# Window attention and gated feed-forward on one core: weight loads ahead of casts, value tiles held back, half turns one to a slot, query copies on ScalarE

## The chip, the core and the metric

The kernel runs on one core of a Trainium2 chip. The metric is the device time of one execution in microseconds. Executions of one kernel agreed within about 1% here (263.0 to 265.9 us for most runs of the kernel before), so differences are read from rounds in which both kernels ran on the same chip. Medians are over all runs of a round; where a slow one is among them, this is said. The changed kernel was timed in one round only, so an experiment is set against it across rounds; the kernel before had medians of 264.65, 264.78, 264.01 and 264.18 us in the four rounds, so less than about 1 us between rounds decides nothing.

## The reference

Four batches of eight heads, 768 positions, 64 columns a head. Each position attends to the first 4 positions and to the last 128. A feed-forward part follows, with a relu gate.

```python
scores = scale * np.matmul(q, k.transpose(0, 1, 3, 2))
keep = is_sink | in_window                  # 4 sinks, window of 128
a = softmax(np.where(keep, scores, -1e9))   # written out in the original
attn = np.matmul(a, v)                      # (4, 8, 768, 64)
x = attn.transpose(0, 2, 1, 3).reshape(3072, 512)
out = (np.maximum(x @ w_gate, 0) * (x @ w_val)) @ w_out    # d_ff = 1536
```

## The kernel before

The feed-forward part of a batch is 24 *slots*: two halves of the positions (g = 0, 1) by twelve column blocks of 128 (m). A slot is one `chunk`: four matmuls for the gate, four for the value, a relu on ScalarE and a product on VectorE (`hT`). Attention work of the same or the next batch is put behind the chunks by a plan: `S` is one group of scores with its exp and mask, `V` the sums, the division and the value product of one pair of heads, `T` the turn of keys and queries to head-dimension-major form, `H` the turn of the second half of batch 0's positions. "V01" is pair 0, part 1 (the second half); the chunks of g = 1 need all four V of part 1.

```python
def chunk(b, g, m):
    gp, vp = G[gvn[0] % 3], G[(gvn[0] + 1) % 3]         # three banks in turn
    ...  # 4 matmuls with wg into gp
    nc.scalar.activation(gs[:], gp[:, 0:CUT], Act.Relu, bias=0.0, scale=1.0)
    ...  # 4 matmuls with wv into vp
    nc.vector.tensor_tensor(h[:, m, c], gs[:], vp[:, 0:CUT], op=Alu.mult)

def V(u, part):
    x = V1(u, part)     # sums with ones
    V3(*x[:3])          # values: vn, tile by tile
    V4(*V2(*x))         # division and product on VectorE, into xT
```

The weights are cast while they are loaded, and GpSimd asks for them; it also casts the value tiles (`vf` to `vn`) and the halves of keys and queries, all in one order. SyncE asks for the float32 tiles. (To *ask* for a load is to issue its DMA.) In the profile's lines `qT` and `kE` are the turned queries and keys, `ee` the exps, `xT` the attention output, `hT` the product of a chunk, `wg` and `wv` the gate and value weights, `g` and `pp` banks of PSUM. L282 are the scores, L298 the sums and the value products, L340 and L345 the gate and value matmuls of a chunk, L131 the casts of value tiles.

```python
cast_v(0, 1)
cast_v(0, 2)
...
cast_half(3, (nc.gpsimd.tensor_copy, nc.scalar.copy))
Sg(U[2], 0)
load_w(0, 2)                    # gate and value weights of blocks 0 and 1
...
load_w(2, 4)
load_half(6)
load_half(7)
for j in (3, 4, 5, 6):          # the value tiles of part 1
    load_v(0, j, 16 if j == 3 else 0)
...
prep[1] += [("half", 6), ("half", 7), ("v", 0, 3), ("v", 0, 4), ("w", 6, 8), ("v", 0, 5), ("v", 0, 6),
            ("w", 8, 10), ("w", 10, 12)]
```

The softmax here doesn't subtract the row's maximum and nothing guards it: scores larger than these inputs give would overflow.

Of the kernel before, what the change touches and what calls it, by code (L numbers as in the profile page):

```python
# [19 lines left out]
def kernel(  # L20
# [12 lines left out]
    nc = tc.nc  # L33
# [19 lines left out]
    vf = const.tile([128, 7, H, 64], F32, name="vf")  # L53
# [66 lines left out]
    def load_v(b, j, r0=0, r1=128):  # L120
        r1 = min(r1, S - VROW[j])

        parts = [(0, 4, 0), (4, 16, VROW[j] + 4), (16, 128, VROW[j] + 16)] if j in (1, 3, 5) else [(0, 128, VROW[j])]
        for a0, a1, s0 in parts:
            a1 = min(a1, r1)
            if r0 <= a0 < a1:
                nc.sync.dma_start(out=vf[a0:a1, j, :, :], in_=v[b, :, s0:s0 + a1 - a0, :].rearrange("h s d -> s h d"))  # L127

    def cast_v(b, j, rows=128, copy=nc.gpsimd.tensor_copy):
        flat = lambda ap: ap.rearrange("p h d -> p (h d)")  # L130
        copy(flat(vn[b % 2][0:rows, j, :, :]), flat(vf[0:rows, j, :, :]))  # L131
# [27 lines left out]
        copy(e[:, 124:892].rearrange("d (i c) -> d i c", c=256)[:, :, 0:4],  # L159
             e[:, 0:4].unsqueeze(1).to_broadcast([128, 3, 4]))  # L160

    def load_w(m0, m1):
        for w, dst in ((moe_w_gate, wg), (moe_w_val, wv)):
            nc.gpsimd.dma_start(out=dst[:, :, m0 * 128:m1 * 128],
                                in_=w.rearrange("(ko ki) n -> ki ko n", ki=128)[:, :, m0 * 128:m1 * 128])

# [64 lines left out]
    def T(u):  # L231
        t = u.i % NT
        tk, tq = two()
        for x, ps in ((kn[u.i % 2], tk), (qn[u.i % 2], tq)):
            for n in range(NR):
                for h in range(2):
                    r = slice(64 * h, 64 * h + 64)
                    nc.tensor.transpose(ps.bitcast(BF16)[r, 64 * n:64 * n + 64], x[r, 64 * n:64 * n + 64], ident[r, r])
        vk, vq = (ps.bitcast(BF16)[:, 0:S].rearrange("d (n p) -> d p n", p=PR) for ps in (tk, tq))
        e = kE[t]  # L240
        to = lambda ap: ap.rearrange("d (p n) -> d p n", n=NR)
        nc.scalar.copy(to(e[:, 0:120]), vk[:, 0:10])
        for i in range(2):
            nc.scalar.copy(to(e[:, 128 + 256 * i:380 + 256 * i]), vk[:, 10 + 21 * i:31 + 21 * i])
        nc.scalar.copy(to(e[:, 640:784]), vk[:, 52:64])
        nc.vector.tensor_copy(to(qT[t][:]), vq)  # L246
        sinks(u, nc.scalar.copy)

    def T_half(c):
# [117 lines left out]
    with tc.manual_schedule():  # L367
        nc.vector.memset(idle[:], 0.0)
        spin(7)
        load_half(0, (nc.sync, nc.scalar))  # L370
        load_half(1, (nc.sync, nc.scalar))
        load_v(0, 0)
        load_v(0, 3, 0, 16)
        load_half(2)
        load_v(0, 1)
        load_v(0, 2)
        for c in range(3, 6):
            load_half(c)
        setup()
        setup2(1)  # L380
        cast_half(0)
        T_half(0)
        spin(2, 1)
        Sg(U[0], 0)
        Sg(U[0], 3)
        cast_half(1)
        T_half(1)
        cast_v(0, 0)
        cast_v(0, 3, 16, nc.vector.tensor_copy)
        x = V1(U[0], 0)  # L390
        v0 = V2(*x)
        Sg(U[1], 0)
        cast_half(2)
        cast_v(0, 1)
        cast_v(0, 2)
        Sg(U[1], 3)
        T_half(2)
        x = V1(U[1], 0)
        v1 = V2(*x)
        V3(*v0[:3])  # L400
        V4(*v0)
        V3(*v1[:3])
        V4(*v1)
        cast_half(3, (nc.gpsimd.tensor_copy, nc.scalar.copy))
        Sg(U[2], 0)
        load_w(0, 2)
        Sg(U[2], 3)
        T_half(3)
        cast_half(4)
        V(U[2], 0)  # L410
        Sg(U[3], 0)
        cast_half(5)
        Sg(U[3], 3)
        load_w(2, 4)
        load_half(6)
        load_half(7)
        for j in (3, 4, 5, 6):
            load_v(0, j, 16 if j == 3 else 0)
        V(U[3], 0)
        T_half(4)  # L420
        setup2(2)
        load_w(4, 6)
        spin(6, 2)
        head[0] = False


        slots = []
        for b in range(B):
            slots += [(b, g, m) for g in range(2) for m in range(FM)]
        plan = [[] for _ in slots]  # L430
        at = {}

        def put(s, y, n):
            st = (y[0], n * NP + int(y[1]), int(y[2]) if len(y) > 2 else 0)
            at[st] = s
            plan[s].append(st)

        for s, w in {0: "S04 S02 H1", 1: "S14 S12", 2: "H2", 3: "S24 S22 H3", 4: "S34 S32", 5: "V01", 6: "V11",
                     7: "V21", 8: "V31"}.items():
            for y in w.split():  # L440
                put(s, y, 0)
        for s, w in {12: "T0", 13: "T1", 14: "S00 S01", 15: "S10 S11", 16: "T2", 17: "S20 S21", 18: "V00",
                     19: "V10 T3", 20: "V20", 21: "S30 S31", 22: "V30 S02"}.items():
            for y in w.split():
                put(s, y, 1)
        for b in range(2, B + 1):
            if b < B:
                w = ("Vp01 Sp12 Vp11 Sp22 Vp21 Sp32 Vp31 Sn00 Sn01 Sn10 "
                     "Vn00 Sn11 Sn20 Vn10 Sn21 Sn30 Vn20 Sn31 Vn30 Sn02")
            else:  # L450
                w = "Vp01 Sp12 Vp11 Sp22 Vp21 Sp32 Vp31"
            for x, y in enumerate(w.split()):
                put(24 * (b - 1) + x // 2 * 2, y[0] + y[2:], b - (y[1] == "p"))
        prep = [[] for _ in slots]
        prep[1] += [("half", 6), ("half", 7), ("v", 0, 3), ("v", 0, 4), ("w", 6, 8), ("v", 0, 5), ("v", 0, 6),
                    ("w", 8, 10), ("w", 10, 12)]
        prep[9] += [("load", 4), ("load", 5), ("load", 6), ("lv", 1)]
        prep[10] += [("kq", 4), ("load", 7), ("kq", 5)]
        prep[13] += [("kq", 6)]
        prep[15] += [("v", 1, j) for j in range(7)]  # L460
        prep[16] += [("kq", 7), ("td", 8), ("wo",)]
        for i in range(ND, len(U)):
            t = at["S", i - NP, 2] + 1
            if i > ND:
                prep[t - 6].append(("td", i))
            prep[t].append(("turn", i))
            prep[at["S", i, 0] - 1].append(("sinks", i))
            assert t < at["S", i, 0] - 2
        for b in range(2, B):
            s0 = at["V", b * NP, 0]  # L470
            prep[s0 - 7].append(("lv", b))
            for j in range(7):
                prep[s0 - 3 + j // 2 if j < 6 else s0].append(("v", b, j))

        f2 = deque()
        for s, (b, g, m) in enumerate(slots):
            for x in prep[s]:
                if x[0] == "kq":
                    cast_kq(U[x[1]])
                elif x[0] == "load":  # L480
                    gate(U[x[1]])
                    load_kq(U[x[1]])
                elif x[0] == "half":
                    cast_half(x[1])
                elif x[0] == "w":
                    load_w(*x[1:])
                elif x[0] == "wo":
                    for c in range(3):
                        load_wo(c)
                elif x[0] == "td":  # L490
                    to_dram(U[x[1]])
                elif x[0] == "turn":
                    turn(U[x[1]])
                elif x[0] == "sinks":
                    sinks(U[x[1]], nc.gpsimd.tensor_copy)
                elif x[0] == "lv":
                    for j in range(7):
                        load_v(x[1], j)
                else:
                    cast_v(*x[1:])  # L500
            chunk(b, g, m)
            for what, i, x in plan[s]:
                if what == "T":
                    T(U[i])
                elif what == "H":
                    T_half(NP + i)
                elif what == "S":
                    Sg(U[i], x)
                else:
                    V(U[i], x)  # L510
            for _ in range(3):
                if f2:
                    f2.popleft()()
            if s == 23:
                f2 += [lambda t=t, mm=mm: ffn2(0, t, mm) for t in range(6) for mm in range(FM)]
            if b > 0 and m == FM - 1:
                f2 += [lambda b=b, t=t, mm=mm: ffn2(b, t, mm) for t in range(3 * g, 3 * g + 3) for mm in range(FM)]
        tail[0] = 1
        while f2:
            f2.popleft()()  # L520
# [35 lines left out]
```

## Time and profile before

| | before |
|---|---|
| median of the first 3 runs | 264.69 us (263.51 to 265.35) |
| profiled span | 261.9 us |
| TensorE busy | 247.7 us (95%) |
| granted TensorE clock | 0.997 |
| first V of part 1 (slot 5) starts | 33.99 us |
| first turn of batch 1 (slot 12) starts | 47.55 us |

In this page each row has one digit for a fortieth of the span (6.5 us): the busy share of TensorE in tenths, and below it the clock that the throttle granted, in tenths of full speed.

```profile
PE   7877899998899999999999999999999999999994
...
PEclk9999999999999999999999999999999999999998
```

Apart from the end, all waits lie in the first 16 slices (the last is at 102.95 us). The first V of part 1, and the casts of the last two value tiles that it uses, timeline of TensorE and of GpSimd:

```profile
33.99 0.54 PE L298 MATMUL pp<-ee,ones 128*64 128x115 bf16 x10
34.38 0.52 PE L298 MATMUL pp<-ee,vn 128*64 128x115 bf16 x10
...
30.34 1.75 POOL L131 CAST vn<-vf 128x512 bf16<-128x512 f32 x2 [1.72 <-DMA vf<-in_v_dram]
```

The casts are done by 32.1, 2 us before V01 starts, and V01 waits for nothing.

### The profile page before, as it was taken

The page shows a single profiled execution, that of the slowest core. Times are in us where ns is not written, and L with a number is a line of the kernel's source. Part 1 is how long each engine was busy: PE and PEld are TensorE (multiplying, and loading weights), DVE is VectorE, ACT ScalarE, POOL GpSimd, SP SyncE. Part 2 cuts the span into 40 slices and gives each one's busy share as a digit, 9 for nine tenths or more (in the row PEclk, how much of TensorE's full clock was granted, in tenths as well). Part 3 has the DMA queues.
Part 4 walks back from the last instruction along what each step waited for, and adds up shares of the span by engine and source line. Part 5 has one row for each costly group of instructions (what it writes and reads, how often), then busy time and mean ns, then how long its engine had stood idle before and what let it go on. Part 6 is the DMA issues. An engine that isn't in the chain of part 4 may idle for free.

```text
span 261.9 us, 5490 instructions
## 1 busy us (share of the span) xinstructions
PE 247.7 (95%) x2143; PEld 140.5 (54%) x2143; DVE 151.2 (58%) x316; ACT 116.5 (44%) x224; POOL 73.0 (28%) x100
## 2 busy tenths in 40 slices
PE   7877899998899999999999999999999999999994
PEld 2454565655555555555555555555555655555441
DVE  7675888487987665657357567667265742323000
ACT  3765742594543454454333464463344233332211
POOL 6791631759960003894000033000000000000000
PEclk9999999999999999999999999999999999999998
DMA  7999997995999969499712393310110011101232
GB/s 192 275 248 191 149 131 194 309 238 56 158 170 155 115 133 203 98 163 145 117 52 62 69 219 85 109 43 0 40 43 7 36 40 40 41 4 40 80 123 80
DMA packets 81266, 30.45 MB, mean 116 GB/s; under 512 B 65368, under 2 KB 77144, under 8 KB 81240
## 3 DMA queue, kind: packets, MB, share of 16 engines
q1 hardware_dynamic: 47944, 21.83, 34.3%
q0 software_dynamic: 32752, 7.87, 34.1%
q8 instruction: 17, 0.28, 0.5%
q10 hardware_dynamic: 544, 0.39, 0.5%
q14 instruction: 9, 0.07, 0.1%
HBM read 28.48 MB, written 9.44 MB: 145 GB/s over the span
## 4 chain that ended last, share of the span: by engine, by line
PE 74%; DMA 8%; DVE 7%; ACT 3%; issue 3%; SPq 2%; POOL 1%; DVEq 0%; ACTq 0%
PE g L360 20%; PE g L340 19%; PE g L345 19%; PE pp L298 7%; DMA vf<-in_v_dram 5%; PE pp L360 4%; PE pp L282 4%; DMA wv<-in_moe_w_val_dram 3%; ACT ee L286 3%; SPq L127 2%; DVE hT L347 2%; DVE t L313 1%; DVE R L315 1%; DVE ee L289 1%; DVE qT L246 1%
## 5 line engine op out<-in xcount | busy, mean ns | idle before, releaser
L347 DVE TENSOR_TENSOR hT<-gs,g 128x384 bf16<-128x384 f32 x96 | 52.8, 550 | 65.5 <-PE g L345 64.7
L340 PE MATMUL g<-xT,wg 128*128 128x384 bf16 x384 | 78.4, 326 | 0.7 <-DVE hT L347 0.5
L345 PE MATMUL g<-xT,wv 128*128 128x384 bf16 x384 | 78.1, 326 | 0.7 <-DMA wv<-in_moe_w_val_dram 0.7
L343 ACT ACTIVATE gs<-g 128x384 f32<-128x384 f32 x96 | 47.4, 494 | 69.1 <-PE g L340 67.2
L360 PE MATMUL g<-wo,hT 128*128 128x512 bf16 x240 | 64.1, 380 | 0.0
L286 ACT ACTIVATE ee<-pp 128x998 bf16<-128x998 f32 (+4 forms) x52 | 45.3, 902 | 34.9 <-PE pp L282 34.8
L340 PEld LDWEIGHTS <-wg 128*128 128x128 bf16 x384 | 36.0, 98 | 32.5 <-issue 2.1
L345 PEld LDWEIGHTS <-wv 128*128 128x128 bf16 x384 | 37.5, 98 | 26.0 <-DMA wv<-in_moe_w_val_dram 1.1
L360 PEld LDWEIGHTS <-hT 128*128 128x128 bf16 x288 | 26.2, 98 | 26.2 <-issue 2.1
L289 DVE TENSOR_TENSOR ee<-ee,msk 128x838 bf16<-128x838 bf16 (+4 forms) x48 | 30.0, 633 | 10.7 <-ACT ee L286 10.6
L131 POOL CAST vn<-vf 128x512 bf16<-128x512 f32 x28 | 18.1, 654 | 39.7 <-DMA vf<-in_v_dram 37.3
L148 POOL DMA_DIRECT2D qd<-in_q_dram x8 | 25.1, 4452 | 0.0
L148 POOL DMA_DIRECT2D kd<-in_k_dram x8 | 22.7, 3910 | 0.3 <-issue 0.3
L282 PE MATMUL pp<-qT,kE 64*128 64x255 bf16 (+6 forms) x240 | 17.2, 246 | 3.7 <-DVE qT L267 1.7
L364 ACT COPY ot<-g 128x512 f32<-128x512 f32 x20 | 11.7, 586 | 18.2 <-PE g L360 17.4
L315 DVE STREAM_TRANSPOSE R<-r 128x384 f32<-128x384 f32 x32 | 18.5, 578 | 1.1
L313 DVE STREAM_TRANSPOSE t<-pp 128x384 f32<-128x384 f32 x28 | 16.2, 580 | 4.1 <-PE pp L298 3.5
L298 PEld LDWEIGHTS <-ones 128*64 128x64 bf16 x288 | 12.6, 109 | 10.4 <-issue 9.8
L323 DVE TENSOR_TENSOR xT<-pp,R 128x384 bf16<-128x384 f32 x28 | 15.6, 557 | 1.0
L282 PEld LDWEIGHTS <-kE 64*128 64x128 bf16 x240 | 8.8, 94 | 11.8 <-issue 8.4
L298 PE MATMUL pp<-ee,ones 128*64 128x115 bf16 (+8 forms) x256 | 14.4, 237 | 0.2
L298 PE MATMUL pp<-ee,vn 128*64 128x115 bf16 (+8 forms) x256 | 13.9, 233 | 0.5 <-POOL vn L131 0.5
(74 smaller groups left out, 129.3 us busy)
## 6 DMA issues: line engine op xcount, KB each, us to landing
out_dram<-ot SPq DMA_DIRECT2D x24, 256.0 KB
vf<-in_v_dram SPq DMA_DIRECT2D x12, 256.0 KB
vf<-in_v_dram SPq DMA_DIRECT2D x12, 224.0 KB
kf<-in_k_dram SPq DMA_DIRECT2D x8, 192.0 KB
wg<-in_moe_w_gate_dram POOLq DMA_DIRECT2D x6, 256.0 KB, 7.2
wv<-in_moe_w_val_dram POOLq DMA_DIRECT2D x6, 256.0 KB, 8.1
kf<-in_k_dram SPq DMA_DIRECT2D x4, 384.0 KB
qf<-in_q_dram SPq DMA_DIRECT2D x4, 384.0 KB
```

Of the source, the lines that this page charges most:

```text
L148: nc.gpsimd.dma_start(out=dst[u.i - ND].rearrange("s (h d) -> s h d", h=2), in_=x[u.b, 2 * u.p:2 * u.p + 2].rearrange("h s d -> s h d"))
L282: nc.tensor.matmul(out=ps[:, h, c0:c1], lhsT=kE[t][64 * h:64 * h + 64, x0:x0 + 128], rhs=qT[t][64 * h:64 * h + 64, q0:q0 + c1 - c0], start ...
L286: nc.scalar.activation(x, ps[:, :, b0:n], Act.Exp, bias=0.0, scale=scale)
L289: nc.vector.tensor_tensor(x, x, msk[:, g, m0:m0 + c1 - c0].unsqueeze(1).to_broadcast([128, 2, c1 - c0]), op=Alu.mult)
L298: nc.tensor.matmul(out=out[64 * h:64 * h + 64, o0:o0 + c1 - c0], lhsT=w(j, h), rhs=ee[u.i % NE][:, g, h, c0:c1], start=i == 0, stop=i == l ...
L313: nc.vector.transpose(out=t1[:], in_=pd[:, 0:CUT])
L315: nc.vector.transpose(out=R[:].rearrange("p (c e) -> p c e", e=32), in_=r[:].unsqueeze(2).to_broadcast([128, CUT // 32, 32]))
L340: nc.tensor.matmul(out=gp[:, 0:CUT], lhsT=wg[:, ko, m * 128:(m + 1) * 128], rhs=x[:, ko, c], start=ko == 0, stop=ko == KO - 1)
L343: nc.scalar.activation(gs[:], gp[:, 0:CUT], Act.Relu, bias=0.0, scale=1.0)
L345: nc.tensor.matmul(out=vp[:, 0:CUT], lhsT=wv[:, ko, m * 128:(m + 1) * 128], rhs=x[:, ko, c], start=ko == 0, stop=ko == KO - 1)
L347: nc.vector.tensor_tensor(h[:, m, c], gs[:], vp[:, 0:CUT], op=Alu.mult)
L360: nc.tensor.matmul(out=op, lhsT=hT[b % 2][:, m, t * 128:(t + 1) * 128], rhs=wo[:, m, :], start=m == 0, stop=m == FM - 1)
```

## The change

The intent: ask for all weights early, because some of their asks stood behind casts that wait for value tiles; hold the value tiles back so that the weights come first; turn each half a slot before it is used; take batch 1's query copies from VectorE; and set its outputs (V00 to V30) further apart. The diff, cut to its core:

```diff
-    def load_w(m0, m1):
+    def load_w(m0, m1, which=(0, 1)):
...
-        nc.vector.tensor_copy(to(qT[t][:]), vq)          # T, batch 1
+        nc.scalar.copy(to(qT[t][:]), vq)
...
         cast_v(0, 1)
+        load_w(0, 2, (0,))
         cast_v(0, 2)
...
-        load_w(0, 2)
+        load_w(0, 2, (1,))
...
-        for j in (3, 4, 5, 6):
-            load_v(0, j, 16 if j == 3 else 0)
...
         load_w(4, 6)
+        cast_half(6)
+        cast_half(7)
...
-        {0: "S04 S02 H1", 1: "S14 S12", 2: "H2", 3: "S24 S22 H3", 4: "S34 S32", 5: "V01", 6: "V11",
-         7: "V21", 8: "V31"}
+        {0: "H1 S04 S02", 1: "H2 S14", 2: "H3 S12", 3: "S24 S22", 4: "S34 S32", 7: "V01", 8: "V11",
+         9: "V21", 10: "V31"}
-        {... 16: "T2", 17: "S20 S21", 18: "V00", ...}
+        {... 16: "T2", 17: "V00", 18: "S20 S21", ...}
...
-        prep[1] += [("half", 6), ("half", 7), ("v", 0, 3), ("v", 0, 4), ("w", 6, 8), ("v", 0, 5), ("v", 0, 6),
-                    ("w", 8, 10), ("w", 10, 12)]
+        prep[0] += [("lv0",), ("w", 6, 8), ("w", 8, 10), ("w", 10, 12), ("v", 0, 3), ("v", 0, 4), ("v", 0, 5),
+                    ("v", 0, 6)]
...      # some casts and loads of batches 1 and 2 are listed a slot earlier or later
+                elif x[0] == "lv0":
+                    for j in (3, 4, 5, 6):
+                        nc.gpsimd.memset(vf[32:33, j, 0, 0:2], 0.0)
+                        load_v(0, j, 16 if j == 3 else 0)
```

The small memset is a gate: SyncE may ask for the tile only after GpSimd has written into it, and GpSimd reaches it only after its earlier work.

More of the change, by code (lines that the diff above doesn't have):

```diff
@@ L160, in sinks @@
              e[:, 0:4].unsqueeze(1).to_broadcast([128, 3, 4]))
-    def load_w(m0, m1):
-        for w, dst in ((moe_w_gate, wg), (moe_w_val, wv)):
+    def load_w(m0, m1, which=(0, 1)):
+        for w, dst in (((moe_w_gate, wg), (moe_w_val, wv))[x] for x in which):
             nc.gpsimd.dma_start(out=dst[:, :, m0 * 128:m1 * 128],
@@ L436, in put @@
             plan[s].append(st)
-        for s, w in {0: "S04 S02 H1", 1: "S14 S12", 2: "H2", 3: "S24 S22 H3", 4: "S34 S32", 5: "V01", 6: "V11",
-                     7: "V21", 8: "V31"}.items():
+        for s, w in {0: "H1 S04 S02", 1: "H2 S14", 2: "H3 S12", 3: "S24 S22", 4: "S34 S32", 7: "V01", 8: "V11",
+                     9: "V21", 10: "V31"}.items():
             for y in w.split():
                 put(s, y, 0)
-        for s, w in {12: "T0", 13: "T1", 14: "S00 S01", 15: "S10 S11", 16: "T2", 17: "S20 S21", 18: "V00",
+        for s, w in {12: "T0", 13: "T1", 14: "S00 S01", 15: "S10 S11", 16: "T2", 17: "V00", 18: "S20 S21",
                      19: "V10 T3", 20: "V20", 21: "S30 S31", 22: "V30 S02"}.items():
@@ L454 @@
         prep = [[] for _ in slots]
-        prep[1] += [("half", 6), ("half", 7), ("v", 0, 3), ("v", 0, 4), ("w", 6, 8), ("v", 0, 5), ("v", 0, 6),
-                    ("w", 8, 10), ("w", 10, 12)]
+        prep[0] += [("lv0",), ("w", 6, 8), ("w", 8, 10), ("w", 10, 12), ("v", 0, 3), ("v", 0, 4), ("v", 0, 5),
+                    ("v", 0, 6)]
         prep[9] += [("load", 4), ("load", 5), ("load", 6), ("lv", 1)]
-        prep[10] += [("kq", 4), ("load", 7), ("kq", 5)]
+        prep[10] += [("kq", 4), ("load", 7)]
+        prep[11] += [("kq", 5)]
         prep[13] += [("kq", 6)]
-        prep[15] += [("v", 1, j) for j in range(7)]
-        prep[16] += [("kq", 7), ("td", 8), ("wo",)]
+        prep[14] += [("v", 1, j) for j in range(7)]
+        prep[15] += [("kq", 7)]
+        prep[16] += [("td", 8), ("wo",)]
         for i in range(ND, len(U)):
@@ L464 @@
             if i > ND:
-                prep[t - 6].append(("td", i))
+                prep[t - 5].append(("td", i))
             prep[t].append(("turn", i))
```

## The prediction

> **What bounds the kernel now.** I read the page first, then TensorE's list of waits, then the timelines of TensorE, GpSimd and VectorE over the first 75 us.
>
> ```profile
> PE 247.7 (95%) x2143; PEld 140.5 (54%) x2143; DVE 151.2 (58%) x316; ACT 116.5 (44%) x224; POOL 73.0 (28%) x100
> ```
>
> TensorE is busy for 247.7 of 261.9 us and its clock is granted in full (0.997). The change removes no matmul, so only idle time of TensorE can be won: 14.2 us. The windowed busy times put 3.9 us of it in the last 22 us (the last outputs leaving) and the rest before 110 us. The list of waits says what ended it:
>
> ```profile
> PE pp L282 <- DVE qT L267: 1.7, 2, 0.9
> PE pp L260 <- ACT ee L286: 1.4, 2, 0.7
> PE g L229 <- DVE warm L172: 1.3, 1, 1.3
> PE pp L282 <- DVE qT L246: 1.0, 2, 0.7
> PE g L298 <- ACT ee L286: 0.9, 2, 0.7
> PE pp L282 <- DVE xT L323: 0.8, 1, 0.8
> PE g L345 <- DMA wv<-in_moe_w_val_dram: 0.7, 1, 0.7
> PE pp L238 <- DVE xT L323: 0.7, 1, 0.7
> PE g L340 <- DVE hT L347: 0.5, 1, 0.5
> PE pp L298 <- POOL vn L131: 0.5, 1, 0.5
> ```
>
> The columns are total, times and longest. The change aims at seven of these: the first value weights (0.74), the half turns' qT (0.79 + 0.95), hT (0.54), batch 1's qT (0.34 + 0.67), and xT twice (0.69 + 0.77). Their sum is 5.5 us; 2% of 264.69 is 5.3. So even a change that erased all of them would only just be faster by 2%.
>
> The trace's places, each line giving start, length and, in brackets, the wait before it:
>
> ```profile
> 19.92 0.81 PE L340 MATMUL g<-xT,wg 128*128 128x384 bf16 x4 [0.17 <-DVE xT L323]
> 21.47 0.82 PE L345 MATMUL g<-xT,wv 128*128 128x384 bf16 x4 [0.74 <-DMA wv<-in_moe_w_val_dram]
> ...
> 25.27 0.51 PE L282 MATMUL pp<-qT,kE 64*128 64x115 bf16 x10 [0.79 <-DVE qT L267]
> ...
> 32.14 0.52 PE L282 MATMUL pp<-qT,kE 64*128 64x115 bf16 x10 [0.95 <-DVE qT L267]
> ```
>
> **What the Trainium skill says.** (1) "DMA: Bandwidth & Descriptors", section "Queues, rings and completion order": each DMA engine takes turns between the queues that have work. The trace agrees: from 15 to 27 us, with value loads on SyncE's queue, the weights' queue starts about 120 KB in a microsecond, and with that queue empty (30 to 32 us) 170 to 195 KB. (2) "PSUM — Partial Sum Buffer", section "PSUM bank collisions raise a hardware error": compilers put a dependency between ScalarE and VectorE on one bank. Here VectorE's qT copy at 49.55 started 0.02 us after ScalarE's last kE copy let go, though VectorE had sat idle for 1.27 us; so moving that copy to ScalarE removes no overlap that exists now. (3) "ScalarE: Activation LUTs", section "What ACT_TABLE_LOAD costs": 186 ns + 0.833 ns an element, back to back about 93 ns less. The trace agrees at 384 columns (0.49 to 0.50 us, formula 0.51), so I estimate 0.83 us for the 768-column copy, 0.73 of it added. VectorE takes 0.96.
>
> **The change part by part.**
>
> *Weights early, value tiles late.* GpSimd works in order:
>
> ```profile
> 9.76 0.62 POOL L131 CAST vn<-vf 128x512 bf16<-128x512 f32 x1 [0.82 <-DMA vf<-in_v_dram]
> 10.68 0.62 POOL L131 CAST vn<-vf 128x512 bf16<-128x512 f32 x1 [0.30 <-DMA vf<-in_v_dram]
> 11.28 0.51 POOL L114 CAST kn<-kf 128x384 bf16<-128x384 f32 x1
> 11.73 0.91 POOL L164 DMA_DIRECT2D wg<-in_moe_w_gate_dram  x1
> 12.63 0.76 POOL L164 DMA_DIRECT2D wv<-in_moe_w_val_dram  x1
> ```
>
> The gate weights' issue (0.91) moves in front of the second cast, which then ends at 10.38 + 0.91 + 0.62 = 11.91 instead of 11.30. That cast is on the path: TensorE's value matmul at 11.35 was let go by it. From there each step waits for the one before (scores, exp, transposes, qT copy, scores, exp, sums, division, xT), without slack that I can find, so the first FFN matmul moves from 19.92 to 20.53: a loss of 0.61. In exchange the value weights come in time. They landed at 21.42, first packet at 14.9, with 660 KB of value tiles and late halves on the other queue meanwhile. With the issue 1.3 us sooner and the value tiles held back to about 20 us I estimate 19 to 20 us, before their use at 20.53 + 0.65 = 21.18. Against 21.47 before, the net gain is 0.3 us.
>
> *Half turns one to a slot.* Each is now issued a slot, or at least one 1.3 us chunk, before its use, and its qT copy stands ahead of the score masks on VectorE. That takes away 0.79 + 0.95 and about 0.1 of a small wait at 28.93. All turns share one bank: the third should wait about 0.15 for the second's qT copy. Net 1.7 us.
>
> *V stages at slots 7 to 10 instead of 5 to 8.* The hT wait of 0.54 (VectorE needs 2.42 us for each V slot, TensorE 2.24) should go, because slot 12 now gives VectorE time. But slots 5 and 6 become bare 1.3 us chunks behind two exps and two masks (0.8 us each on ScalarE), where I expect waits of about 0.2. And the value tiles, 3104 packets of 256 bytes at 245 a microsecond beside the weights, take 12.7 us. Asked for behind the last half casts, at 20 to 21, with 1.3 us to the first packet, they land at about 34 to 34.5 and are cast by 35; their first use is at about 35.2. I put 0.3 us of expected wait on that. Net 0.
>
> *Batch 1's qT on ScalarE, outputs a slot apart.* Walking slots 12 to 22 with the trace's durations: S01's wait of 0.34 goes. S11 gets a wait of 0.3, since two turns of 0.73 us extra put the exps late. T2's qT wait of 0.67 and T3's xT wait of 0.69 go. But the pair of banks alternates, and S21 now comes two users after V00: V00's division starts after hT of slot 17, which waits for ScalarE's relu behind T2's copies, and ends 3.5 us after V00 starts, where S21 is due after 2.4. A wait of 1.1 arises. V20 gets 0.1, and S31 keeps some 0.85 of its 0.77. Removed 2.47 (and some 0.15 of unlisted wait), arisen 2.35: net 0.2.
>
> *Afterwards.* Batch 1's loads start with slot 9, which comes some 3.6 us earlier while T0 comes 2 earlier, so loads, casts and the transfers for batch 2 gain some slack. The wait of 0.49 at 102.95, for a value tile, will probably shrink: 0.3. After that TensorE is never idle until the end, and nothing there changes.
>
> Sum: 0.3 + 1.7 + 0.0 + 0.2 + 0.3 = 2.5 us, so 264.69 - 2.5 = 262.2.
>
> **The rivals.**
> - *The waits only change their names.* For it: each of VectorE, ScalarE and GpSimd is in order, and I found five new waits. The value tiles could be later than I think (they wait for the half loads, which now share the DMA engines with the weights 1.3 us longer); each microsecond counts in full, as would a V00 wait of 2 us. Then the gain falls to 0 to 1: 263.7 to 264.7. Against it: the half turns' gain needs nothing but order.
> - *Everything targeted goes.* If V00's division is not late and GpSimd's detour has slack, the gain is 5.5 to 6: 258.7 to 259.2. Against it are the in-order walk above and the wait of the value matmul at 11.35.
> - *ScalarE becomes the bound in slots 12 to 22.* My sum for it there is 19 us (eleven relus of 0.45, eight exps of 0.93, four turns of 1.75) in 24 us; over the page it is at 44%. It makes single waits, not a bound; worth at most 1 us.
> - *The weights are hidden anyway.* Only the first value weights are waited for now; asking earlier for columns 768 to 1535 brings nothing by itself.
>
> **Range and chances.** The listed gains are bounded by 6 and my new waits could be off by 2 either way: 260.0 to 264.3. The three runs of before spread over 1.8 us, which is part of that range. Faster by 2% needs under 259.4, that is nearly every wait gone: 0.07. Slower by 2% needs 5.3 us of new waits: 0.02.
>
> **What would show it.** Right: no wait on wv; no wait of L282 on qT; the second value cast ending near 11.9 and the first FFN matmul near 20.5; slot 5 some 2 us earlier than 32.59; the first batch 1 transposes near 45.3 instead of 47.55; a new wait of L282 on xT of about 1 us near 57 to 60. Wrong: the value matmul near 11.35 not moved, a wait of L298 on vn of over 1 us near 35, a new wait on weights, or any new idle time after 110 us.

## The result and the profile after

| | before | after |
|---|---|---|
| median | 264.65 us (4 runs) | 267.80 us (267.09 to 268.13, 4 runs) |
| profiled span | 261.9 us | 266.3 us |
| granted TensorE clock | 0.997 | 0.987 (0.987 to 0.993 over the runs) |
| first V of part 1 | 33.99 (slot 5) | 34.79 (slot 7) |
| first turn of batch 1 | 47.55 | 52.49 |

The ratio is 1.012, with a 95% interval of 1.008 to 1.016. Ratios here compare the fast runs of the two kernels in the same rounds, as the record gives them; they are not quite the ratios of the medians. The changed kernel is slower by 1.2%: within 2%, but above the prediction's range (260.0 to 264.3) and on the other side of zero.

The page after, the same two rows:

```profile
PE   7779949999889999999999999999999999999994
...
PEclk9999995999999999999999999999999999999999
```

A hole has opened in the sixth slice (33 to 40 us), and in the seventh the clock was half. TensorE's list of waits after, its first three rows:

```profile
PE pp L298 <- POOL vn L131: 3.9, 3, 3.5
PE pp L282 <- DVE xT L323: 1.9, 2, 1.0
PE pp L260 <- ACT ee L286: 1.4, 2, 0.7
```

The waits on wv and on qT that the change aimed at are gone. A wait on `vn`, the cast value tiles, stands on top. TensorE's timeline after shows where:

```profile
34.79 0.54 PE L298 MATMUL pp<-ee,ones 128*64 128x115 bf16 x10
35.17 0.45 PE L298 MATMUL pp<-ee,vn 128*64 128x115 bf16 x6
39.10 0.33 PE L298 MATMUL pp<-ee,vn 128*64 128x144 bf16 x2 [3.48 <-POOL vn L131]
39.66 0.23 PE L298 MATMUL pp<-ee,vn 128*64 128x20 bf16 x2 [0.22 <-POOL vn L131]
39.82 1.46 PE L340 MATMUL g<-xT,wg 128*128 128x384 bf16 x4
41.07 1.49 PE L345 MATMUL g<-xT,wv 128*128 128x384 bf16 x4
```

V01 does its sums and its first three tiles, then waits 3.48 and 0.22 us for the last two. And the chunk behind the wait is slow: its gate and value groups start 1.25 us apart, where they start about 0.65 apart in chunks at full clock. The trace's clock record has TensorE at half rate from 38.69 to 45.52 us; the work before the wait had ended at 35.62.

GpSimd's timeline after shows why the tiles are late:

```profile
21.33 0.19 POOL L501 MEMSET vf<- 1x2 f32 x4
21.46 0.74 POOL L164 DMA_DIRECT2D wg<-in_moe_w_gate_dram  x1
...
25.11 0.80 POOL L164 DMA_DIRECT2D wv<-in_moe_w_val_dram  x1
29.41 0.72 POOL L131 CAST vn<-vf 128x512 bf16<-128x512 f32 x1 [3.50 <-DMA vf<-in_v_dram]
34.65 0.61 POOL L131 CAST vn<-vf 128x512 bf16<-128x512 f32 x1 [4.52 <-DMA vf<-in_v_dram]
38.44 1.16 POOL L131 CAST vn<-vf 128x512 bf16<-128x512 f32 x2 [3.18 <-DMA vf<-in_v_dram]
```

The gate opens at 21.33, and six weight loads are asked for right behind it. The trace's packets: the first value packet moves at 23.86; from 28 to 34 us the value tiles' queue starts 222 packets in a microsecond and the weights' queue 245; and the last of the 3104 value packets moves at 37.93.

Stretch by stretch, from the times of the same instructions in the two traces:

| stretch | before | after | difference |
|---|---|---|---|
| to the first V of part 1, counted with two more chunks before (2 x 1.30) | 36.59 | 34.79 | -1.80 |
| from there to the first turn of batch 1, less those chunks before | 10.96 | 17.70 | +6.74 |
| batch 1's turns and outputs, to slot 22's chunk | 23.56 | 23.33 | -0.23 |
| the rest | 190.77 | 190.48 | -0.29 |
| sum | 261.88 | 266.30 | +4.42 |

The +6.74 is made of the two waits (3.70), a new wait of 0.44 for the last V of part 1 at the first chunk of the second half, less the wait of 0.54 on hT that went, and 3.14 left over. The half clock accounts for most of that: from 39.66 to 45.52 TensorE worked 5.86 us at half rate, half of which, 2.9 us, is lost.

### The profile page after: what moved, and what is told of

It is laid out like the page before. It is cut to its first block, busy times and chain, and to the rows that moved or that the text cites. A ratio compares the mean times of both kernels' runs of the same rounds, so it can differ in the third digit from the quotient of the medians.

```text
span 266.3 us, 5491 instructions
## 1 busy us (share of the span) xinstructions
PE 251.0 (94%) x2143; PEld 141.2 (53%) x2143; DVE 147.1 (55%) x312; ACT 119.0 (45%) x228; POOL 73.9 (28%) x104
## 4 chain that ended last, share of the span: by engine, by line
PE 73%; DMA 13%; DVE 4%; ACT 3%; SPq 3%; POOL 2%; issue 1%; ACTq 0%; POOLq 0%
PE g L360 19%; PE g L340 19%; PE g L345 19%; DMA vf<-in_v_dram 8%; PE pp L298 7%; DMA qf<-in_q_dram 5%; PE pp L360 4%; PE pp L282 3%; SPq L127 3%; PE pp L238 1%; POOL vn L131 1%; DVE t L313 1%; ACT qT L246 1%; DVE R L315 1%; DVE hT L347 1%
## 5 line engine op out<-in xcount | busy, mean ns | idle before, releaser
L340 PE MATMUL g<-xT,wg 128*128 128x384 bf16 x384 | 79.9, 331 | 0.6 <-DVE xT L323 0.6
L345 PE MATMUL g<-xT,wv 128*128 128x384 bf16 x384 | 78.9, 329 | 0.1
L340 PEld LDWEIGHTS <-wg 128*128 128x128 bf16 x384 | 36.2, 98 | 32.5 <-issue 2.0
L289 DVE TENSOR_TENSOR ee<-ee,msk 128x838 bf16<-128x838 bf16 (+4 forms) x48 | 29.3, 619 | 8.1 <-ACT ee L286 7.8
L282 PE MATMUL pp<-qT,kE 64*128 64x255 bf16 (+6 forms) x240 | 17.7, 246 | 2.2 <-DVE xT L323 1.9
L298 PE MATMUL pp<-ee,vn 128*64 128x115 bf16 (+8 forms) x256 | 14.7, 239 | 3.9 <-POOL vn L131 3.9
L298 PEld LDWEIGHTS <-ones 128*64 128x64 bf16 x288 | 12.7, 111 | 10.7 <-issue 10.1
L298 PEld LDWEIGHTS <-vn 128*64 128x64 bf16 x288 | 12.7, 114 | 5.5 <-POOL vn L131 5.4
L298 PE MATMUL pp<-ee,ones 128*64 128x115 bf16 (+8 forms) x256 | 14.8, 242 | 0.1
```

The source lines that it names most:

```text
L282: nc.tensor.matmul(out=ps[:, h, c0:c1], lhsT=kE[t][64 * h:64 * h + 64, x0:x0 + 128], rhs=qT[t][64 * h:64 * h + 64, q0:q0 + c1 - c0], start ...
L289: nc.vector.tensor_tensor(x, x, msk[:, g, m0:m0 + c1 - c0].unsqueeze(1).to_broadcast([128, 2, c1 - c0]), op=Alu.mult)
L298: nc.tensor.matmul(out=out[64 * h:64 * h + 64, o0:o0 + c1 - c0], lhsT=w(j, h), rhs=ee[u.i % NE][:, g, h, c0:c1], start=i == 0, stop=i == l ...
L340: nc.tensor.matmul(out=gp[:, 0:CUT], lhsT=wg[:, ko, m * 128:(m + 1) * 128], rhs=x[:, ko, c], start=ko == 0, stop=ko == KO - 1)
L345: nc.tensor.matmul(out=vp[:, 0:CUT], lhsT=wv[:, ko, m * 128:(m + 1) * 128], rhs=x[:, ko, c], start=ko == 0, stop=ko == KO - 1)
```

## The experiments

The theories: **A**, the gate makes the tiles late, whatever the weights do. **B**, the early weights crowd the tiles out, wherever the tiles are asked for. And on the clock: it fell because TensorE was idle for 3.5 us, or for another reason.

### The tiles asked for early again

```diff
         load_half(7)
+        for j in (3, 4, 5, 6):
+            load_v(0, j, 16 if j == 3 else 0)
...
-        prep[0] += [("lv0",), ("w", 6, 8), ...
+        prep[0] += [("w", 6, 8), ...
```

> The changed kernel with one part undone: the four value tiles of batch 0's second half are asked for where the kernel before asked for them, not behind a memset on GpSimd. Theory A (the late ask is the cause): the wait of 3.48 + 0.22 us at the first V of part 1 goes, with it the half-clock stretch of 6.8 us that cost some 3 us, the value tiles land at 30 to 32 us, and the time is 267.8 - 3.7 - 3.0 = 261.1; a wait of up to 0.4 on the first value weights may come back, so 261.0 to 261.8. Rival B (the weights asked for early crowd the tiles out wherever they are asked for): the tiles still land after 36 us and the time stays above 265.

Measured: 262.46 us, 0.992 of before (0.988 to 0.996), clock 0.997 or more. No wait on the tiles at V01 and no half clock, so 5.3 us came back. But the tiles did not land at 30 to 32: the last value packet moved at 35.18 and the last cast ended at 36.2. They were in time only because V01 came at 37.1, after TensorE had waited for weights, 0.31 us in slot 0 and then in two later slots:

```profile
30.77 0.82 PE L345 MATMUL g<-xT,wv 128*128 128x384 bf16 x4 [0.21 <-DMA wv<-in_moe_w_val_dram]
...
35.07 0.82 PE L345 MATMUL g<-xT,wv 128*128 128x384 bf16 x4 [0.97 <-DMA wv<-in_moe_w_val_dram]
```

So A had the time nearly right and the landing wrong, and B the landing nearly right and the time wrong: the early weights do crowd the tiles, but here the waits that this makes add up to 1.5 us and none is long. The expected time was missed by 0.7 us.

### Dummy matmuls in the wait

```diff
     def V(u, part):
         x = V1(u, part)
+        if u.i == 0 and part == 1:
+            spin(16, 3)
```

> The changed kernel with 16 dummy matmuls of 512 columns (some 0.22 us each, 3.5 us) between the sums and the value matmuls of the first V of part 1, where TensorE waits 3.48 us. It shortens no wait; it keeps TensorE busy in it. If the half clock after the wait is caused by TensorE's idleness, the clock stays full and the time falls by some 3 us, to 264.8. If the clock drop has another cause (a limit from all activity), it stays at 0.987 and the time is 267.8 or a little more.

Measured: 265.62 us (three runs at 265.6 and one at 268.13), 1.007 of before, clock 0.997 to 1.0. Busy times of two stretches, changed kernel and this one; the first columns are the stretch, its length, TensorE's busy time and its instructions, and the third from the end is the granted clock:

```profile
33.40:39.80 6.40, 2.70 (x29) 1.56 (x27) 1.11 (x2) 0.49 (x1) 1.77 (x3) 0.91 0.79 108
39.80:45.60 5.80, 5.80 (x36) 3.11 (x35) 3.92 (x9) 0.89 (x5) 0.45 (x1) 0.51 0.44 148
```

```profile
33.40:39.80 6.40, 6.24 (x48) 3.30 (x47) 1.71 (x5) 0.76 (x2) 1.28 (x3) 1.00 0.63 86
39.80:45.60 5.80, 5.80 (x81) 3.88 (x79) 5.56 (x12) 0.97 (x5) 0.10 (x1) 1.00 0.76 232
```

In the second stretch TensorE is busy throughout in both, but does 36 instructions at clock 0.51 and 81 at full clock (the counts mix large and small ones). Nothing but dummy work was added, and all four runs have a clock of 0.997 or more where all four of the changed kernel have 0.993 or less: the clock fell because TensorE was idle. Two limits: in this profiled run the tiles came 1.8 us sooner, so that without the dummies the wait would have been some 2.3 us (an estimate: from 35.0, when the first three tiles' products would have ended, to the next cast's end at 37.25), and not 3.5; and two fast runs of the kernel before, not profiled, also have a low mean clock (0.991 and 0.987), for a reason that no trace here shows. The time fell by 2.2 us by the medians, not 3. From the chunk behind V01 to the first turn of batch 1 it took 11.76 us instead of 12.67; without its waits (2.02 against 0.44) 9.74 instead of 12.23. So the half clock cost 2.5 us there, but 1.6 of it came back as waits: VectorE's division for V31 and a relu on ScalarE that stood behind a gated load of batch 1 (0.77) were next in line. In the traces the other part of the gain is tiles that landed sooner in that run (the last casts started at 36.64 instead of 38.44) and a head 0.3 us shorter.

### The last weights in the old order, tiles still late

```diff
-        prep[0] += [("lv0",), ("w", 6, 8), ("w", 8, 10), ("w", 10, 12), ("v", 0, 3), ("v", 0, 4), ("v", 0, 5),
-                    ("v", 0, 6)]
+        prep[0] += [("lv0",), ("v", 0, 3), ("v", 0, 4), ("w", 6, 8), ("v", 0, 5), ("v", 0, 6),
+                    ("w", 8, 10), ("w", 10, 12)]
```

> The changed kernel with the value tiles still behind the memset, but the last six weight loads in the order of before (after casts that wait for tiles). Theory A says the ask at 21.4 us alone makes the tiles late: first packet still near 23.9, landing at best near 31 to 32 because the weights' queue runs dry near 27; a wait of 0 to 1 us at the first V of part 1 and up to 1 us on the weights of slots 6 and 8: 261.5 to 263.5. Rival B (crowding by the early weights is what costs) expects the same gain here as from asking for the tiles early, about 261. If this one stays near 267, neither crowding nor order matters, only the memset.

Measured: 265.09 us (263.67 to 265.69), 1.001 of before. Over the range that A gave and over B's 261, but 2.7 us under the changed kernel. GpSimd's timeline in this kernel:

```profile
20.37 0.19 POOL L501 MEMSET vf<- 1x2 f32 x4
27.37 1.63 POOL L131 CAST vn<-vf 128x512 bf16<-128x512 f32 x2 [6.81 <-DMA vf<-in_v_dram]
28.95 0.74 POOL L164 DMA_DIRECT2D wg<-in_moe_w_gate_dram  x1
...
30.42 1.57 POOL L131 CAST vn<-vf 128x512 bf16<-128x512 f32 x2
```

The last cast starts by 31.0, some 10.6 us after the gate; in the changed kernel it took 17.7 (21.33 to 39.00). The last value packet moved at 28.64, earlier than in the kernel before (29.76). So the gate alone does not make the tiles late, and A is wrong about the cause. What is now late are the weights of slot 6, asked for behind a cast that waits for a tile; TensorE waited 0.85 and 0.81 us for them. Two of the four runs had a clock of 0.994; the profiled one was the fastest and had 1.0, so what those two lost is not shown.

### Both undone

```diff
# the two edits above together: tiles early, last six weight loads in the old order
```

> The changed kernel with both undone: tiles asked for early, last six weights in the order of before. It fills the square of the two. Theory A: 261.0 to 262.0, like undoing the late ask alone. If early tiles and late weights are both needed, this one is faster than each by over 1 us.

Measured: 262.59 us, 0.992 of before (0.987 to 0.997): above A's range by 0.6 us, and no faster than with early tiles alone. With the result and the three runs the square is full; the time in brackets is that of the last value packet in the profiled run:

| median us, ratio to before (last value packet) | weights early | weights in the old order |
|---|---|---|
| tiles late | 267.80, 1.012 (37.93 us) | 265.09, 1.001 (28.64 us) |
| tiles early | 262.46, 0.992 (35.18 us) | 262.59, 0.992 (29.03 us) |

The columns show what delays the tiles: the early weights, by 6 us with early tiles and 9 us with late ones. The gate adds 2.7 us to the landing when the weights are early and nothing when they are not. Each landing is from one run: in the run with dummy matmuls, whose loads are those of the changed kernel, the last value packet moved at 36.57 and not 37.93, so the gate's share may be as little as 1.4 us, while 6 and 9 stand clear of that. With early weights it is the last few packets that drag: the last 133 of 3104 took 3.0 us in the changed kernel and 4.6 with early tiles, against 0.9 and 1.6 with the weights in the old order. Why those few wait so long is not shown. The first use is due at about 35.2 us. Crowding alone brings the tiles just to it; crowding and gate bring them well past it, and only there is the wait long enough for the clock. Late tiles with the old order lose in another way, through the weights that are asked for behind their casts.

### The gate moved 3 us sooner

```diff
         load_w(4, 6)
+        for j in (3, 4, 5, 6):
+            nc.gpsimd.memset(vf[32:33, j, 0, 0:2], 0.0)
+            load_v(0, j, 16 if j == 3 else 0)
         cast_half(6)
...
-        prep[0] += [("lv0",), ("w", 6, 8), ...
+        prep[0] += [("w", 6, 8), ...
```

> The changed kernel with the memsets that gate the value tiles moved ahead of the last two half casts (about 19.2 us instead of 21.4); weights still early. If the tiles' lateness follows the ask (alternating packets at a fixed pace), they land about 2.1 us sooner, near 36.2, and the waits at the first V of part 1 fall from 3.7 to about 1.6 us. If a wait of 1.6 is too short for the clock to drop, the half-clock stretch goes too: 267.8 - 2.1 - 2.9 = 262.8. If the clock drops after it all the same: 265.7. A rival, that the weights' queue sets the landing and the ask does not, expects 267 or more.

Measured: 263.26 us, 0.997 of before (0.992 to 1.001), clock 0.998 or more. In the profiled run the gate opened at 18.06, 3.3 us sooner than in the changed kernel, and the last cast started at 35.61 instead of 39.00, 3.4 us sooner: from the changed kernel to this one the landing follows the ask. TensorE did not wait for the tiles at all, because V01 itself was at 36.45; it had waited for weights before:

```profile
22.05 0.82 PE L345 MATMUL g<-xT,wv 128*128 128x384 bf16 x4 [0.75 <-DMA wv<-in_moe_w_val_dram]
...
34.40 0.82 PE L345 MATMUL g<-xT,wv 128*128 128x384 bf16 x4 [0.96 <-DMA wv<-in_moe_w_val_dram]
```

What the tiles gained the weights gave up, with the DMA engines serving both. The last value packet moved at 35.14 (37.93 in the changed kernel). It did not move sooner with the tiles asked for at 13.99 and no gate (35.18, above), so asking still earlier than 18 us brought nothing, and the rival is right to that extent. But two waits under 1 us leave the clock alone, where one of 3.5 does not. The time was near the 262.8 that I had given for a full clock, though by another way than expected.

### The half turns alone

```diff
-        {0: "S04 S02 H1", 1: "S14 S12", 2: "H2", 3: "S24 S22 H3", 4: "S34 S32", ...
+        {0: "H1 S04 S02", 1: "H2 S14", 2: "H3 S12", 3: "S24 S22", 4: "S34 S32", ...
```

> The kernel before with one part of the change alone: the half turns one to a slot, ahead of the scores that use them. The prediction's step says the two waits on qT in slots 1 and 4 (0.79 and 0.95 us) and a small one go and one of 0.15 us arises: 1.7 us faster, 264.7 - 1.7 = 263.0. A rival, that the freed time is only waited for later (VectorE's backlog in the V slots, or the value tiles at the first V of part 1 near 32 us), expects 264.2 to 264.7 and a longer wait on hT or vn.

Measured: 262.57 us against 264.01 (263.95 without one slow run), 0.994 (0.990 to 0.998): 1.4 us faster by the medians and 1.6 by the ratio; 1.7 were predicted. In the traces it took 12.51 us instead of 14.07 from the first FFN matmul to the first V of part 1, so 1.6 less; the profiled run, the slowest of six, lost it again elsewhere. The waits of L282 on the qT of L267 (1.7 us before) are gone from the list. No wait on the tiles arose at the first V of part 1; a wait for a value tile of batch 2 near 102 us grew from 0.49 to 0.88.

### Batch 1's part alone

```diff
-        nc.vector.tensor_copy(to(qT[t][:]), vq)
+        nc.scalar.copy(to(qT[t][:]), vq)
...
-        17: "S20 S21", 18: "V00"
+        17: "V00", 18: "S20 S21"
```

> The kernel before with batch 1's query copies on ScalarE and V00 ahead of S20 and S21, nothing else. The prediction's walk says 2.5 us of waits go and 2.35 arise: waits of about 1 us on xT before S21 and before S31, no waits on qT; 0.2 us faster, 264.5. A rival, that the copy on ScalarE frees VectorE and the outputs a slot apart end their waits, expects up to 2 us, 262.7 to 263.5.

Measured: 264.08 us against 264.01, 0.999 (0.995 to 1.004): the same. TensorE's timeline in these slots:

```profile
56.16 0.39 PE L282 MATMUL pp<-qT,kE 64*128 64x255 bf16 x4 [0.17 <-ACT ee L286]
...
63.65 0.39 PE L282 MATMUL pp<-qT,kE 64*128 64x255 bf16 x4 [0.97 <-DVE xT L323]
...
71.86 0.39 PE L282 MATMUL pp<-qT,kE 64*128 64x255 bf16 x4 [0.97 <-DVE xT L323]
```

The waits that the prediction's walk had named are there: S11 0.17 (0.3 predicted), S21 0.97 (1.1), S31 0.97 (0.85). Four waits of 2.47 us became three of 2.11.

### The V stages back in slots 5 to 8

```diff
# on top of "both undone"
-        7: "V01", 8: "V11", 9: "V21", 10: "V31"
+        5: "V01", 6: "V11", 7: "V21", 8: "V31"
```

> The changed kernel with early tiles and weights in the old order (262.6), and the V stages of part 1 back in slots 5 to 8. If moving them to slots 7 to 10 costs (a chunk of the second half waits 0.8 us for the last of them, where before waited 0.54 for hT), this is 0.2 to 0.4 us faster: 262.2 to 262.4, with a wait of about 0.5 on hT in place of 0.8 on xT. If the move is what gave the tiles time, a wait on vn over 0.5 us shows near 32 us and the time is over 263.

Measured: 262.68 us, 0.993 of before (0.989 to 0.998), so not to be told from the 262.59 with slots 7 to 10. The expected exchange took place (hT 0.55 instead of xT 0.80), but that run also waited 0.94 for weights in slot 2 and 0.83 for a value tile of batch 2, which the other did not. At this size the runs do not decide.

### A joined version, and its old order of outputs

```diff
# on top of "both undone"
-        load_w(0, 2, (0,))
         cast_v(0, 2)
+        load_w(0, 2)                    # both, ahead of the half cast that has slack
...
-        7: "V01", 8: "V11", 9: "V21", 10: "V31"
+        5: "V01", 6: "V11", 8: "V21", 9: "V31"
...
-        prep[10] += [("kq", 4), ("load", 7)]
+        prep[10] += [("kq", 4)]
+        prep[12] += [("load", 7)]
```

> A candidate: early tiles, the first weights asked for right after the second value cast and ahead of a half cast that has slack, the V stages in slots 5, 6, 8 and 9, and the last gated load two slots later. Expected: no wait of the value matmul near 11.4 us (0.6 us won), no wait on xT at the first chunk of the second half (0.8 won), a wait of 0 to 0.4 us on the first value weights: 262.6 - 1.2 = 261.4. If the wait near 11.4 had slack behind it, only 0.8 is won and the first FFN matmul stays near 20.6.

Measured: 262.01 us, 0.991 of before (0.987 to 0.995). The waits on hT and xT around slot 12 are gone and the value matmul near 11.4 us no longer waits: from the first sums to the first FFN matmul it took 12.04 us, against 12.86 in the changed kernel and 12.31 before. Waits of 0.70 and 0.41 us on a value tile of batch 2 near 101 us took 0.6 more than the 0.49 before.

> The joined candidate (262.0) with batch 1's outputs back in the old order (S20 and S21 in slot 17, V00 in slot 18), the query copies still on ScalarE. It separates the two halves of that part of the change. Without VectorE's copies before it V00's division may end sooner, and the turn T3, not S21, is second after V00 on the pair of banks: the wait there should be 0.2 to 0.7 instead of 0.97, S31 keeps some 0.8: 0.3 to 0.8 us faster, 261.2 to 261.7. If the order was what helped, it is slower than the joined candidate: over 262.2.

Measured, with S20 and S21 back in slot 17 and V00 in slot 18: 261.51 us with one slow run among the six, 261.27 without it; 0.989 of before (0.984 to 0.993). In batch 1 it waits 0.17 + 0.47 + 0.69 + 0.82 = 2.15 us, against 2.11 with the other order. So the order of outputs makes no difference that these runs show, and the two joined versions, timed in different rounds, cannot be told apart. Both beat the kernel before by about 1%, and, across rounds, the changed kernel by about 2%.

## Why the prediction was wrong

- **The first FFN matmul.** Right: the second value cast ended at 11.97 (11.91 predicted), the value matmul behind it started at 12.03, and the first FFN matmul came at 20.60 (20.53). The wait on the first value weights went, as said. (Two small slips in the working: the waits aimed at are eight, in six rows of the list, not seven; and the first packet at 14.9 was the gate weights', the value weights' came at about 17.5.)
- **The half turns.** Right: 1.4 to 1.6 us when done alone.
- **Slot 5 and the first V of part 1.** Right in time: 30.51 and 34.79, 1.8 us ahead of before. Up to here the changed kernel did what the prediction says.
- **The value tiles. This step failed.** The prediction: asked for "at 20 to 21, with 1.3 us to the first packet, they land at about 34 to 34.5 and are cast by 35", and "I put 0.3 us of expected wait on that". Its own terms add up to 34.0 to 35.0, not 34.5, and each was too small: the gate opened at 21.33 and the ask came at 21.44, the first packet took 2.4 us instead of 1.3, and the 3104 packets took 14.1 us instead of 12.7. The pace was not what failed: the first 2971 packets took 11.1 us, 269 in a microsecond where 245 were assumed. The last 133 took 3.0 us, and no term stood for them. The last cast started at 39.00, and TensorE waited 3.70 us where 0.3 was put down. (The prediction's own sign of being wrong, "a wait of L298 on vn of over 1 us near 35", came true.) The experiments add what the landing hangs on: with the six last weights asked for later, the same tiles behind the same gate moved in 5.2 us (23.44 to 28.64). The prediction had the crowding in its sum and never asked what it was worth to avoid it. Against a first use at about 35.2 the sum had a margin of 0.2 us, and its error was 4. A margin of that size under a sum of three estimates deserved several tenths of probability of a long wait, not 0.3 us.
- **The clock. Missing altogether.** No step asked what a wait of several microseconds does to TensorE's clock. The Trainium skill has it: "TensorE: Matmul & The Clock Gate", section "HAM oscillation — how this bites in real kernels", gives the rule "no PE-idle gaps >~3.4µs". The trace agrees in the main: in the wait of 3.48 us the clock fell to half, waits of up to 1.25 us (in the run with dummies) left it full, and with dummy matmuls in the wait it stayed full. By the record it fell 3.07 us after TensorE's last work (35.62 to 38.69), so a little less than the page's figure was enough here; where between 1.25 and 3.07 us the limit lies no run shows. So the step's error counted almost twice: 3.7 us of waiting and 2.5 to 2.9 of half clock.
- **The V stages moved.** The net of 0 was near, but not for its reason: the hT wait of 0.54 went as said, and a wait on xT that I had not seen came, of 0.44 us here and 0.80 to 1.25 in the experiments with the same slots, because the first chunk of the second half needs the last V.
- **Batch 1 and afterwards.** Right: 0.23 and 0.29 us won, 0.2 and 0.3 predicted; alone, batch 1's part measured as nothing. Why VectorE's query copy had started only 0.03 us after ScalarE's last key copy is not shown: the kernel puts keys and queries of a turn into two different banks.
- **The rival** "The value tiles could be later than I think" is what happened, but it was given 1 us or so, and the rival on weights ("asking earlier ... brings nothing by itself") missed that asking earlier takes packets from whatever is asked for at the same time. With the tiles early the change measures 262.46 us, where 262.2 was predicted; that is in part luck, since 1.5 us of waits on weights, which the prediction did not have, stand in it. As it stands the change is slower.

## What to carry to other kernels

When loads are put in an order of need, look for the one that the reorder puts last and add up its landing: when the ask can happen, the time to the first packet with the queues full, packets by pace, and the stragglers at the end; then ask for several microseconds of margin, not tenths. Asking for other loads earlier is not free: here it put the landing of the tiles back by 6 to 9 us. A load that is held back should not have big loads asked for right behind it. And a long TensorE wait can cost more than its length: here 3.7 us of waiting brought 2.5 to 2.9 us of lost half clock after it, where waits of up to 1.25 us brought none. Where such a wait can't be avoided, dummy matmuls can keep the clock, though the next waits in line may take much of the gain (1.6 of 2.5 us here).

## What the Trainium skill lacked or had wrong

- "DMA: Bandwidth & Descriptors", section "Queues, rings and completion order", says that engines take turns between queues by packet, but not what a queue of small packets loses by it: from 28 to 34 us of the changed kernel, with both queues full, 222 packets of the value tiles and 245 of the weights started in a microsecond, which was 57 KB for the tiles (256 bytes a packet in the trace) and 125 KB for the weights (512 bytes as written).
- The same page, section "Latency and other measured facts", gives some 0.6 us to the first byte for loads that SyncE asks for. In the trace after it was 1.1 us from the first ask to the first packet (0.82 to 1.91), 1.0 for batch 1's first load (41.90 to 42.90), and 2.4 with the weights' queue full (21.44 to 23.86).
- "TensorE: Matmul & The Clock Gate", section "What's actually happening", has the full clock back after at least one busy window of about 3.4 us and says that the windows run freely, but not that nearly two can pass. Here the clock stayed at half for 6.83 us, and TensorE worked without a break for the last 5.86 of them before it was full again. That fits two windows of the page's length with the wait ending inside the first; no second case here tests it.
